# Local attention fused with a squared-ReLU layer: scores of four tiles joined in pairs, and a new order of work

## The chip, the core and the metric

The kernel runs on one core of a Trainium2 chip. A core has TensorE (PE; its weight loads have a row of their own, PEld), VectorE (DVE), ScalarE (ACT), GpSimd (POOL), SyncE (SP) and 16 DMA engines. Each engine takes its instructions in the order in which the program lists them, and waits on semaphores of the others. The metric is device time in microseconds, the median of several executions. Before the change it is 212.19 us (five runs, 211.66 to 212.37).

## The reference

For each of 4 batches and 8 heads (768 positions, head size 64), attention with a window, followed by a two-layer network over all 3072 rows:

```python
scores = scale * np.matmul(q, k.transpose(0, 1, 3, 2))
keep = is_global | is_local          # first 8 columns, or 0 <= row - column < 96
scores = np.where(keep, scores + bias[None], -1000000000.0)
a = np.exp(scores - max)             # then divided by its row sum
attn = np.matmul(a, v)               # -> x: 3072 rows of 512
r = np.maximum(x @ w_in, 0.0)        # w_in 512 x 2048
out = (r * r) @ w_out                # w_out 2048 x 512
```

## The kernel before, in words

**Tiling.** There are 24 tiles of 128 rows (six in each batch, numbered 0 to 23) and 12 blocks of two tiles each. A row sees its own tile, the tile to its left and the eight global columns, which a small DVE copy puts into the first columns of the left tile's keys (line 612, and line 683 for v). A batch's first tile (0, 6, 12, 18) has no left tile.

**Attention of a tile.** Queries and keys are loaded by POOL (line 211; q, k and v of a tile are three transfers that share POOL's queue), and transposed: on PE for tiles 0 to 5 (line 398, copied out of PSUM by lines 326 and 328), by a DMA transpose that SP issues from tile 6 on (line 422). Scores (line 485, `emit_sc`) are matmuls with a contraction of 64, one head each. Even and odd heads lie in the two halves of the array's rows, so the array is split, and an even and an odd head run side by side. A first tile has 8 of these matmuls and fills 2 PSUM banks; any other has 16 and fills 4. Then ACT takes the exponential (line 551, one instruction for each bank), DVE multiplies by mask and slope (line 576), PE multiplies by v (line 638, "pv", in two halves of four heads), DVE divides by the row sum (lines 665 and 666, "norm"), and x is transposed, by PE (line 701) for tiles below 8 and by a DMA transpose from SP (line 725) after that.

**The layer.** Block b and step s (eight of them) make one s1: 8 matmuls (line 753) into a PSUM bank hT. ACT applies the ReLU (line 774), DVE squares (line 786), and s2 adds it to the output tiles of the block (line 826, two matmuls for each step and tile). Finished tiles are copied out (lines 326 and 328) and stored by SP (line 865).

**PSUM.** Two of the eight banks hold s2's sums. The other six are one ring, taken in turn by scores, pv, transposes and s1. A PE operation that takes a bank waits until what was in it six banks ago has been read.

**What sets the order.** Each operation is entered in a `Plan` with a cost for its engine, its dependencies and a key. `Plan.run` places them one after the other, always the one that could start first, with 0.01 us for each unit of key (`URGE`), and the instructions are written to the engines in that order. The constants steer the keys: `SHIFT` by kind of operation, or by kind and tile, block or step; `LEADS` by how much a tile's attention runs ahead of the layer. `JOIN` holds pairs (tile, first group): such a tile's scores are no operation of their own, but are appended to the score operation before them (`joint`), so that they are issued in one stretch, which has the dependencies of both and takes the banks of both. `STEP` says after which s1 (counted through all blocks) a tile's scores may come; `HOLD` keeps the next s1 behind them.

Before the change, `JOIN` has tiles 15, 16, 18, 20, 21 and 23; their partners are the parts before them. Scores of tiles 6, 7, 11 and 12 are four stretches.

Of the kernel before, what the change touches and what calls it, by code (L numbers as in the profile page):

```python
# [21 lines left out]
class Plan:  # L22
# [8 lines left out]

    LAG = {"PE": 0.25, "ACT": 0.26, "DVE": 0.2, "SP": 0.6, "POOLQ": 0.8, "DMAQ": 1.2, "DMA": 0.0}
    URGE = 0.01
    SHIFT = {'T': -13, 'sc': -2.5, 'exp': -26, 'pv': -13, 'norm': -17, 'trx': -5, 'xT': 32, 'gk': -38, 'gv': -45, 'mul': -39, 'kl': 24, 's1': -3.5, 'relu': 8, 'sq': -13, 's2': -1.25, 'st': -30, ('mul', 4): 12, ('tr', 5): 18, ('T', 5): 8, ('norm', 5): -22, ('sc', 6): 16, ('pv', 6): 46, ('mul', 7): 29.5, ('gk', 7): -13, ('trx', 7): 12, ('sc', 8): -4, ('pv', 8): 9, ('norm', 9): -10, ('pv', 11): 14, ('pv', 12): 48, ('sc', 13): -14, ('pv', 14): 30, ('mul', 15): 17, ('norm', 17): 4, ('norm', 18): -36, ('exp', 19): -7, ('exp', 20): 14, ('pv', 20): 34, ('sc', 22): 10, ('s1', 2): -2.5, ('s1', 3): -32, ('sq', 3): 4, ('s1', 5): 9, ('s1', 6): 23.5, ('s1', 7): 34, ('s1', 8): -10, ('s2', 0): 7.5, ('s2', 2): -4, ('s2', 3): -27, ('s2', 4): 7.5, ('s2', 5): 22, ('s2', 6): 14, ('s2', 7): -4, ('s2', 8): -10, ('s2', 9): -8, ('s2', 10): -2}

    def shift(self, name):
        early = name[-1 if name[0] in ("T", "tr") else 1]
        return self.SHIFT.get(name[0], 0.0) + self.SHIFT.get((name[0], early), 0.0)

# [65 lines left out]
def kernel(  # L105
# [49 lines left out]
    def const(shape, dt, name):  # L155
        return consts.tile(shape, dt, name=name, tag=name)
# [18 lines left out]
    pbt = const([P, 2, P], FP32, "pbt")  # L175
    pbw = const([P, 2, P], FP32, "pbw")
    plan = Plan()
    LEADS = {5: 29.5, 6: 59, 7: 21, 8: 15, 9: 40, 10: 38, 11: 24, 12: 46, 13: 0, 14: 22, 15: 1, 16: -27, 17: 18, 18: -20, 19: 20, 20: 33, 22: 28, 23: 8}
    SAFE = {j: 1.6 for j in range(6, 12)} | {14: 4.2, 15: 3.2, 16: 3.5}
    SAFEX = {9: 1.5, 11: 1.5, 13: 2.5}  # L180


    SETS = {1: [(0,), (1,)], 2: [(0,), (1,)], 3: [(0,), (1,)], 15: [(0,), (1,)], 20: [(0,), (1,)], 23: [(0,), (1,)]}
    JOIN = {(21, 0), (16, 0), (23, 0), (18, 0), (20, 0), (15, 0)}
    COPY = [14, 15, 19, 20, 22]
    BEHIND = {}
    HOLD = ((6, 0), (19, 0))
    STEP = {(17, 0): 58, (19, 0): 68, (4, 0): -7, (6, 0): 16, (11, 0): 24, (12, 0): 37}
    JGATE = 11
    NHS = 14  # L190
    NWARM = 8
# [68 lines left out]
    def emit_ones(e, js):  # L260
        for j in js:
            nc.vector.memset(v_sb[j][:, :, D : D + 1], 1.0)
# [38 lines left out]
    for g in range(NFIRST + 2, NT, 6):  # L301
        js = range(g, min(g + 6, NT))
        o = plan.op(
            ("ones", g), {"DVE": 0.2}, lambda e, js=js: emit_ones(e, js),
            key=-1.0, ready=15.0,
        )
# [40 lines left out]
    kl = [const([P, NPAIR, P], BF16, f"kl_{i}") for i in range(2 if COPY else 0)]  # L347
# [8 lines left out]
    for j in range(NT):  # L356
        b, t = divmod(j, TPB)
        first = t == 0
        need = 8 * (j // 2)
        base = need - LEADS.get(j, LEAD) + 4 * (j % 2)  # L360
        if (j, 0) in JOIN:
            base -= 4
# [28 lines left out]
        for n in range(2) if j < JQK else ():  # L391
            users = []

            def emit_tr(e, j=j, n=n, fp=fp):
# [9 lines left out]
            tr = plan.op(  # L404
                ("tr", n, j), {"PE": 0.5 if fp else 0.24}, emit_tr,
                deps=[land["qk"[n], j]], key=base, takes=(*G, [users]),
            )
# [12 lines left out]
        if j >= JQK:  # L420
            def emit_dT(e, j=j, T_=T_):
# [5 lines left out]
            T = plan.op(  # L427
                ("T", j), {"SP": 1.3}, emit_dT,
                deps=[land["q", j], land["k", j], xT_op[j - 3]] + ku, key=base - 6,
            )  # L430
            T = plan.op(("moved", j), {"DMAQ": 1.2}, None, deps=[T])
            qk_users[slot(j)].append(T)
            if j in SAFE:

                T = plan.op(("seen", j), {"DMA": SAFE[j]}, None, deps=[T])
# [6 lines left out]
        mul, mul_users = {}, {}  # L442
# [55 lines left out]
        for gs in SETS.get(j, [tuple(range(groups))]):  # L498
            n = 8 * len(gs)
            sc_users = busers[2 * gs[0] : 2 * gs[-1] + 2]  # L500
            if (j, gs[0]) in JOIN:

                o, also, taken = joint
# [16 lines left out]
            if j < NBIAS:  # L520
# [6 lines left out]
            o = plan.op(  # L527
                ("sc", j, gs[0]), {"PE": 0.2 + 0.029 * n},
                lambda e, gs=also, f=emit_sc: f(e, gs), deps=[*deps, bias],
                key=base + 1 + 2 * gs[0], takes=takes,  # L530
            )
# [91 lines left out]
        norm = []  # L623
# [170 lines left out]
    for o in plan.ops:  # L794
        if o["name"][0] == "sc":
            j = o["name"][1]
            n = STEP.get(o["name"][1:], 4 * j - LEAD)
            if n >= 0 and j >= NFIRST:
                o["deps"].append(s1_ops[n // NSTEP, n % NSTEP])
                if o["name"][1:] in HOLD:  # L800
                    n += 1
                    s1_ops[n // NSTEP, n % NSTEP]["deps"].append(o)

    for blk in range(NBLK):
# [9 lines left out]
        for s, sub, half in order2:  # L814
# [5 lines left out]
            def emit_s2(e, blk=blk, s=s, sub=sub, half=half, w=w, cols=cols, own=own):  # L820
# [15 lines left out]
            o = plan.op(  # L836
                ("s2", blk, s, sub), {"PE": 0.43 * w / d_model}, emit_s2,
                deps=[d, land["wout", s]] + users[-1:],
                key=8 * blk + s + 2.0 + (0 if not last else 8 * sub + 8 * (half or 0)),
                takes=((*G, [users]) if own else ("acc", NACC, [users])) if s == 0 else None,  # L840
            )
# [6 lines left out]
            if s == NSTEP - 1:  # L848
# [14 lines left out]
                def emit_st(e, blk=blk, sub=sub, half=half, cols=cols):  # L863
# [7 lines left out]
                st = plan.op(  # L871
                    ("st", blk, sub), {"SP": 0.4}, emit_st,
                    deps=[ev, s1_ops[NLATE, 0] if blk < NLATE - 2 else None],
                    key=8 * blk + s + 9.0,
                )
                st = plan.op(("stored", blk, sub), {"DMAQ": 1.4}, None, deps=[st])
# [40 lines left out]
```

## Time and profile before

| | us |
|---|---|
| median of 5 runs | 212.19 |
| the profiled execution, its own time | 211.98 |
| its span, first to last instruction | 210.2 |
| PE busy | 203.2 |
| DVE busy | 143.2 |
| ACT busy | 119.4 |
| s1 matmuls (line 753), 768 | 94.2 |
| s2 matmuls (line 826), 376 in the records | 90.1 |
| exponentials (line 551), 78 with their mask on DVE | 40.4 |

The profile gives instructions with start and duration, the idle time of an engine ahead of an instruction with the engine that ended it ("waited for"), and a chain that is followed back from the last instruction. TensorE's granted clock was 1.00 in the whole span. PE's matmuls overlap, so that a row's duration is longer than what it adds: the step from the start of one matmul to that of the next is what counts. In the records, s1's matmuls follow each other at 109 ns, s2's at 216 ns, pv's at 29.5 ns. The program has 1984 matmuls and the profile 1960 records: where one of s2's is missing, a hole of 216 ns shows that is none.

### The profile page before, as it was taken

To read this page: it belongs to the slowest core of one execution; us is meant where nothing else is said; L and a number is where in the kernel's file an instruction comes from. 1 tells how busy PE (TensorE), PEld (TensorE's weight loads), DVE (VectorE), ACT (ScalarE), POOL (GpSimd) and SP (SyncE) were. 2 spreads that over 40 slices of the span, in tenths; PEclk is the share of its full clock that TensorE was granted. 3 is DMA by queue.
4 is the path that set the end of the run, shared out by engine and by line. 5 is a ranking of instruction groups with operands and counts; after the bars stand their busy time and mean duration, and the time that the engine had idled before them with its cause. 6 is when DMAs were issued, how large, how long until landed. Compare 5 with 4: busy or idle time off the path is not lost.

```text
span 210.2 us, 4998 instructions
## 1 busy us (share of the span) xinstructions
PE 203.2 (97%) x1960; PEld 142.0 (68%) x1984; DVE 143.2 (68%) x372; ACT 119.4 (57%) x222; POOL 73.8 (35%) x91
## 2 busy tenths in 40 slices
PE   7998999999999999999999999999999999999993
PEld 3686877666566856866856577587756766766862
DVE  7799688522887877884877684586786845944630
ACT  6886688134663754554754672755677436833531
POOL 8997765440637238213903150405500000000000
PEclk9999999999999999999999999999999999999999
DMA  8999999999799999999997979999973710410202
GB/s 127 149 177 187 184 191 200 176 179 223 76 172 135 201 120 162 190 145 138 159 155 76 218 72 97 143 133 113 136 133 75 176 27 3 125 27 3 100 0 100
DMA packets 112615, 27.32 MB, mean 130 GB/s; under 512 B 103248, under 2 KB 109648, under 8 KB 112592
## 3 DMA queue, kind: packets, MB, share of 16 engines
q0 software_dynamic: 79200, 13.37, 86.6%
q1 hardware_dynamic: 33392, 13.64, 33.6%
q8 instruction: 15, 0.25, 0.5%
q14 instruction: 8, 0.07, 0.1%
HBM read 27.26 MB, written 6.29 MB: 160 GB/s over the span
## 4 chain that ended last, share of the span: by engine, by line
PE 85%; POOL 5%; DMA 4%; DVE 2%; issue 1%; ACT 1%; POOLq 0%
PE acc L826 39%; PE hT L753 37%; PE sc L485 5%; PE po L638 4%; DMA win<-in_moe_w_in_dram 4%; POOL qk L211 3%; POOL v L211 2%; DVE x L666 1%; POOL win L211 1%; PE tr L398 0%; DVE hs L786 0%; DVE rs L665 0%; PE trx L701 0%; DVE at L576 0%; ACT hr L774 0%
## 5 line engine op out<-in xcount | busy, mean ns | idle before, releaser
L753 PE MATMUL hT<-xT,win 128*128 128x256 bf16 x768 | 94.2, 273 | 0.8 <-DMA win<-in_moe_w_in_dram 0.6
L826 PE MATMUL acc<-wout,hs 128*128 128x512 bf16 (+1 forms) x376 | 90.1, 370 | 1.3 <-DVE rs L665 0.2
L774 ACT ACTIVATE hr<-hT 128x512 f32<-128x512 f32 x96 | 57.3, 605 | 55.2 <-PE hT L753 46.8
L753 PEld LDWEIGHTS <-win 128*128 128x128 bf16 x768 | 73.5, 98 | 18.3 <-DMA win<-in_moe_w_in_dram 1.0
L786 DVE TENSOR_TENSOR hs<-hr 128x512 bf16<-128x512 f32 x96 | 65.1, 687 | 23.2 <-ACT hr L774 22.4
L826 PEld LDWEIGHTS <-hs 128*128 128x128 bf16 x400 | 36.8, 98 | 29.8
L551 ACT ACTIVATE esc<-sc 128x512 bf16<-128x512 f32 x78 | 40.4, 608 | 13.6 <-PE sc L485 13.0
L211 POOL DMA_DIRECT2D qk<-in_q_dram x23 | 20.7, 900 | 70.8 <-DMA qkT<-qk 53.4
L576 DVE TENSOR_TENSOR at<-esc,E 128x512 bf16<-128x512 bf16 x78 | 31.8, 422 | 8.6 <-ACT esc L551 6.3
L211 POOL DMA_DIRECT2D v<-in_v_dram x24 | 22.0, 915 | 1.4 <-DMA win<-in_moe_w_in_dram 1.0
L666 DVE TENSOR_TENSOR x<-po,rs 128x256 bf16<-128x256 f32 x48 | 20.4, 424 | 1.7
L211 POOL DMA_DIRECT2D qk<-in_k_dram x23 | 20.6, 899 | 0.5 <-DMA win<-in_moe_w_in_dram 0.5
L326 ACT COPY o<-acc 128x512 f32<-128x512 f32 (+1 forms) x20 | 11.2, 579 | 15.1 <-PE acc L826 15.0
L638 PEld LDWEIGHTS <-at 128*128 128x128 bf16 x352 | 15.6, 98 | 4.8 <-ACT at L551 0.2
L638 PE MATMUL po<-v,at 128*128 128x65 bf16 x352 | 17.3, 193 | 0.1
L665 DVE RECIPROCAL rs<-po 128x4 f32<-128x4 f32 x48 | 8.6, 178 | 10.4 <-PE po L638 9.8
L485 PEld LDWEIGHTS <-qkT 64*128 64x128 bf16 x312 | 9.5, 94 | 6.2 <-issue 5.5
L485 PE MATMUL sc<-qkT 64*128 64x128 bf16 x192 | 12.9, 219 | 0.1
L485 PE MATMUL sc<-qkT,qkT 64*128 64x128 bf16 x120 | 8.7, 216 | 0.0
L328 DVE COPY o<-acc 128x512 f32<-128x512 f32 x5 | 3.5, 692 | 6.9 <-PE acc L826 6.8
L612 DVE COPY qkT<-qkT 128x32 bf16<-128x32 bf16 x11 | 3.0, 271 | 5.8 <-PE sc L485 5.8
L211 POOL DMA_DIRECT2D win<-in_moe_w_in_dram x8 | 6.2, 806 | 1.4 <-issue 0.6
(45 smaller groups left out, 71.7 us busy)
## 6 DMA issues: line engine op xcount, KB each, us to landing
out_dram<-o SPq DMA_DIRECT2D x23, 256.0 KB, 3.7
v<-in_v_dram POOLq DMA_DIRECT2D x24, 128.0 KB, 6.4
qk<-in_q_dram POOLq DMA_DIRECT2D x23, 128.0 KB, 4.6
qk<-in_k_dram POOLq DMA_DIRECT2D x23, 128.0 KB, 5.8
win<-in_moe_w_in_dram POOLq DMA_DIRECT2D x8, 256.0 KB, 7.9
wout<-in_moe_w_out_dram POOLq DMA_DIRECT2D x8, 256.0 KB, 9.3
qkT<-qk SPq DMA_TRANSPOSE x18, 5.3
plain<-in_q_dram SPq DMA_DIRECT2D x1, 256.0 KB, 3.3
```

What stands on the lines that cost most here:

```text
L211: nc.gpsimd.dma_start(out=dst, in_=src)
L326: nc.scalar.copy(dst, src)
L485: nc.tensor.matmul(out=tiles["sc", j, odd, g][:, at, :], lhsT=left[j - 1][half, pair, :] if kt else qkT[j % NKT][half, 1, pair, :], rhs=qk ...
L551: nc.scalar.activation(out=esc, in_=tiles.pop(("sc", j, odd, g)).rearrange("p a c -> p (a c)"), func=Act.Exp, scale=scale,)
L576: nc.vector.tensor_mul(at, tiles.pop(("esc", j, odd, g)), bias)
L638: nc.tensor.matmul(out=po[:, hi, :], lhsT=tiles["at", j, odd, g][:, at * P : (at + 1) * P], rhs=v_sb[kj][:, h, :], start=(i == 0), stop=(i ...
L665: nc.vector.reciprocal(rs, po[:, :, D : D + 1])
L666: nc.vector.tensor_tensor(out=x[:, 4 * hf : 4 * hf + 4, :], in0=po[:, :, :D], in1=rs.to_broadcast([P, 4, D]), op=Alu.mult,)
L753: nc.tensor.matmul(out=hT[:, c, :], lhsT=w_in_sb[s][:, kt, c * P : (c + 1) * P], rhs=tiles["xT", blk][:, kt, :], start=(kt == 0), stop=(kt ...
L774: nc.scalar.activation(hr, tiles.pop(("hT", blk, s)), Act.Relu)
L786: nc.vector.tensor_mul(hs, hr, hr)
L826: nc.tensor.matmul(out=tiles["acc", blk, sub, half], lhsT=hs[:, c, sub * P : (sub + 1) * P], rhs=w_out_sb[s][:, c, cols], start=(s == 0 an ...
```

## The change

It touches constants alone. `JOIN` gains (7, 0) and (12, 0): scores of tile 7 follow those of tile 6, and those of tile 12 follow those of tile 11, in one stretch of 24 matmuls that takes all six banks of the ring. With it come other values in `SHIFT`, `LEADS`, `HOLD` and `STEP`, so that the whole order of work is another.

```diff
-    SHIFT = {'T': -13, 'sc': -2.5, 'exp': -26, 'pv': -13, 'norm': -17, 'trx': -5, 'xT': 32, 'gk': -38, 'gv': -45, 'mul': -39,
...
+    SHIFT = {'T': 47, 'sc': -5.25, 'pv': -2, 'norm': 26.5, 'trx': -2, 'xT': 51, 'gk': 42, 'gv': -127.5, 'mul': 24,
...
-    LEADS = {5: 29.5, 6: 59, 7: 21, 8: 15, 9: 40, 10: 38, 11: 24, 12: 46, 13: 0, 14: 22, 15: 1, 16: -27, 17: 18, 18: -20, 19: 20, 20: 33, 22: 28, 23: 8}
+    LEADS = {3: 51, 4: 17, 5: 16, 6: 27, 8: 2, 9: 20, 10: 42, 11: 47, 12: 0, 14: 0, 15: 7.5, 16: 34, 17: 46, 20: 28, 21: 15, 23: 56}
...
-    JOIN = {(21, 0), (16, 0), (23, 0), (18, 0), (20, 0), (15, 0)}
+    JOIN = {(7, 0), (12, 0), (21, 0), (16, 0), (23, 0), (18, 0), (20, 0), (15, 0)}
...
-    HOLD = ((6, 0), (19, 0))
-    STEP = {(17, 0): 58, (19, 0): 68, (4, 0): -7, (6, 0): 16, (11, 0): 24, (12, 0): 37}
+    HOLD = ((10, 0),)
+    STEP = {(4, 0): -7, (12, 0): 37, (5, 0): -2, (10, 0): 29, (13, 0): 30, (23, 1): 81}
```

Both programs have the same instructions on PE, SP and POOL, and POOL's stand in the same order. One copy of an output tile and one of an x tile go from DVE to ACT. In the new order PE has 21 stretches of scores in place of 24: the two that `JOIN` takes away, and one in the loading phase, where the two halves of tile 3's scores now stand side by side.

More of the change, by code (lines that the diff above doesn't have):

```diff
@@ L33 @@
     URGE = 0.01
-    SHIFT = {'T': -13, 'sc': -2.5, 'exp': -26, 'pv': -13, 'norm': -17, 'trx': -5, 'xT': 32, 'gk': -38, 'gv': -45, 'mul': -39, 'kl': 24, 's1': -3.5, 'relu': 8, 'sq': -13, 's2': -1.25, 'st': -30, ('mul', 4): 12, ('tr', 5): 18, ('T', 5): 8, ('norm', 5): -22, ('sc', 6): 16, ('pv', 6): 46, ('mul', 7): 29.5, ('gk', 7): -13, ('trx', 7): 12, ('sc', 8): -4, ('pv', 8): 9, ('norm', 9): -10, ('pv', 11): 14, ('pv', 12): 48, ('sc', 13): -14, ('pv', 14): 30, ('mul', 15): 17, ('norm', 17): 4, ('norm', 18): -36, ('exp', 19): -7, ('exp', 20): 14, ('pv', 20): 34, ('sc', 22): 10, ('s1', 2): -2.5, ('s1', 3): -32, ('sq', 3): 4, ('s1', 5): 9, ('s1', 6): 23.5, ('s1', 7): 34, ('s1', 8): -10, ('s2', 0): 7.5, ('s2', 2): -4, ('s2', 3): -27, ('s2', 4): 7.5, ('s2', 5): 22, ('s2', 6): 14, ('s2', 7): -4, ('s2', 8): -10, ('s2', 9): -8, ('s2', 10): -2}
+    SHIFT = {'T': 47, 'sc': -5.25, 'pv': -2, 'norm': 26.5, 'trx': -2, 'xT': 51, 'gk': 42, 'gv': -127.5, 'mul': 24, 'kl': 38.5, 'relu': 25.5, 'sq': 30, 's2': -5, 'o': 61, 'st': 78, ('mul', 3): 28, ('tr', 4): 10, ('xT', 5): -22, ('sc', 6): 14, ('pv', 7): -4, ('norm', 7): -17, ('trx', 7): -3, ('sc', 8): -12, ('pv', 8): -18, ('pv', 10): 45, ('sc', 11): 12, ('pv', 12): -50, ('sc', 13): 17, ('sc', 14): 6, ('pv', 14): 10, ('norm', 14): -28, ('sc', 15): -21, ('exp', 15): 20, ('exp', 16): 83, ('mul', 16): 92, ('norm', 16): -9, ('sc', 17): 32, ('pv', 17): 28, ('pv', 21): 9.5, ('pv', 22): -10, ('norm', 22): 8, ('s1', 2): -8.5, ('sq', 2): -10, ('relu', 3): 24, ('sq', 3): -82, ('s1', 5): 6, ('s1', 6): 30, ('sq', 6): 6, ('s1', 7): -6, ('sq', 7): -92, ('relu', 8): 40, ('s1', 9): -2, ('s1', 10): -10, ('s2', 0): 7.5, ('s2', 2): 1, ('s2', 4): -15, ('s2', 5): 37, ('s2', 6): -5, ('s2', 7): -3, ('s2', 9): 4.5, ('s2', 11): 30}
     def shift(self, name):
```

## The prediction

> **What bounds the kernel now.** I read the clock first (1.00 throughout), then PE's row in the slices, PE's waits, and PE's timeline around the score stretches.
>
> ```profile
> span 210.2 us, 4998 instructions
> ...
> PE   7998999999999999999999999999999999999993
> ```
>
> PE is full from the second slice to the last but one. The view of waits, cut to PE, lists everything that it waited for:
>
> ```profile
> PE warm L271 <- DVE zero L259: 1.2, 1, 1.2
> PE hT L753 <- DMA win<-in_moe_w_in_dram: 0.6, 1, 0.6
> PE tr L398 <- DMA qk<-in_k_dram: 0.2, 1, 0.2
> PE acc L826 <- DVE rs L665: 0.2, 1, 0.2
> PE acc L826 <- DVE qkT L612: 0.2, 1, 0.2
> ```
>
> The first three lie before 20 us. The last two are holes of one s2 matmul (216 ns) where the profile lacks a record, so they are no waits. The last true wait ends here, in PE's timeline; its columns are start, length, instructions:
>
> ```profile
> 18.64 1.05 PE L753 MATMUL hT<-xT,win 128*128 128x256 bf16 x8 [0.62 <-DMA win<-in_moe_w_in_dram]
> 19.52 0.39 PE L701 MATMUL trx<-ident,x 128*128 128x128 bf16 x4
> 19.98 1.05 PE L753 MATMUL hT<-xT,win 128*128 128x256 bf16 x8
> ```
>
> These are s1 of block 0, steps 2 and 3, each held by its piece of w_in. By the records step 3's piece lands at 19.93; PE is done with the transposes at 19.74, so it stands 0.24 us. From 19.98 to the last s2 (207.0) I checked each start against the one before it at the rates of 109, 216, 56 and 29.5 ns: beyond holes of missing records nothing is left, except one cost that comes with each stretch of scores. So the end is set by 19.98 plus PE's work, plus the last copy and store (207.03 to 210.2).
>
> **The price of a stretch.** A stretch of 16 (tile 7) and one of 8 (tile 6), with the rows around them:
>
> ```profile
> 56.02 0.59 PE L826 MATMUL acc<-wout,hs 128*128 128x512 bf16 x2
> 56.54 0.23 PE L485 MATMUL sc<-qkT 64*128 64x128 bf16 x2
> ...
> 56.94 0.22 PE L485 MATMUL sc<-qkT,qkT 64*128 64x128 bf16 x2
> 57.10 0.40 PE L701 MATMUL trx<-ident,x 128*128 128x128 bf16 x4
> ```
>
> ```profile
> 49.70 1.04 PE L753 MATMUL hT<-xT,win 128*128 128x256 bf16 x8
> 50.67 0.40 PE L485 MATMUL sc<-qkT 64*128 64x128 bf16 x8
> 51.00 1.47 PE L826 MATMUL acc<-wout,hs 128*128 128x512 bf16 x6
> ```
>
> The two s2 matmuls from 56.02 are done at 56.02 + 2 x 0.216 = 56.45, the next full-array work starts at 57.10: 0.65 us for 16. For 8: 49.70 + 8 x 0.109 = 50.57, to 51.00: 0.43. The records, to the ns, give 0.648, 0.425, and 0.872 for the six stretches of 24. So eight more cost 0.224, and a stretch costs 0.425 - 0.224 = 0.20 for going in and out; 0.011 comes on top, because the first matmul after a stretch is that much slow. **One stretch less is worth 0.21 us**, if it was on PE's full part.
>
> **The change part by part.**
>
> 1. *Two stretches less after 19.98.* The built orders, laid side by side, have 17 stretches there before and 15 after: 6 with 7, and 11 with 12, are one each. 2 x 0.21 = 0.42 us saved. Counts on PE are the same and the rates too.
>
> 2. *One stretch less before 19.98* (tile 3's halves). Its 0.21 us ends in the wait for w_in: POOL's list is the same, so step 3's piece lands at 19.93 again. Gain 0. If that cover were gone, by an earlier landing, up to 0.2 more; if the new order there made PE late, a loss. That order puts all 18 small memsets ahead of the second half of tile 2's norm (in the profile six take 0.27 us, so 0.81). By the rows (mask 0.34 apart, reciprocal 0.2, norm 0.34), tile 3's x is ready near 19.2, and PE wants it at 19.51: 0.3 spare. Taken: 0.
>
> 3. *The added wait: a joined stretch needs both tiles' keys and all six banks, and everything on PE queues behind it.* Keys: counting the new order's work from 19.98, the stretch 6+7 stands at 52.2; the DMA transpose of tile 7 lands at 50.2 in the records, 2 us earlier. 11+12 stands at 85.9; tile 12's transpose landed at 82.3. Banks: the last s1 ahead of 6+7 ends 3.1 us before it, ahead of 11+12 1.3 us; a ReLU takes 0.61. Taken: 0.
>
> 4. *After the joined stretch* six exponentials stand on ACT. The six stretches of 24 of the old order show the case: at 119.47 PE goes on with three s2 steps (1.3 us, no ring bank) and starts s1 at 120.77 without a gap, while ACT works through the exponentials:
>
> ```profile
> 119.12 2.56 ACT L551 ACTIVATE esc<-sc 128x512 bf16<-128x512 f32 x5 [1.02 <-PE sc L485]
> ```
>
> That is 0.51 us for each bank. The new order has the same three s2 steps behind both joined stretches. Without that cover PE would wait for the first bank until 119.12 + 0.60, some 0.3 us in each stretch, 0.6 in all. Here a rule speaks against the change: the Trainium skill, TensorEngine Tiling (Array Packing), section PSUM Bottleneck, says that tiling speeds up TensorE but not the evacuation of PSUM, and that the PSUM copy may become the bottleneck. Were PE to wait for all six banks, this would make 6 x 0.51 - 1.3 = 1.8 us a stretch, 3.5 in all; the rows show one bank is enough at a time. Taken: 0.
>
> 5. *The rest of the order.* Shortest way from s1 over ReLU and square to its s2: 1.84 us of PE work lie between (block 7, step 7), 1.94 before (block 11, step 7). It needs 0.60 + 0.69 and hand-offs, 1.35 to 1.5 us. With the queues of ACT and DVE laid out by the same rows (exponential 0.53, mask 0.34, norm 0.54, square 0.61, start to start), pv of tiles 12, 19, 20 and 22 and an s2 of block 8 are spared by 0.03 to 0.2 us. Bounds: nothing, or 0.1 to 0.2 us at up to four places, 0.8 at most. I take 0, as the old order's shortest one shows no wait.
>
> 6. *SP and the DMA queues.* SP has the same 61 issues; from block 6 on, stores stand singly between transposes instead of in pairs. A store waits for its copy out of PSUM and holds what is queued behind it: key transposes of tiles 19 and 21 among it, which then still have 17 and 12 us until their scores. What PE waits for here is x: from the last pv of a block's second tile to the block's first s1 over norm, SP and the DMA. PE work between these (start to start) in blocks 4 to 11: before 7.6, 9.6, 11.1, 7.7, 5.7, 6.8, 13.2, 6.3; after 7.4, 7.2, 10.2, 7.7, 6.5, 6.5, 6.3, 9.8. The smallest grows from 5.7 to 6.3. In the records SP issues 1.15 us after that pv starts (86.70 to 87.85, block 5). The landing takes what this row says (us min/median/max, x transposes):
>
> ```profile
> DMA to landing us min/median/max: 2.4/3.7/7.5
> ```
>
> Where the loads are over, it takes 2.4 to 3.6 by the records (blocks 9 to 11). Blocks 4 and 5 lie where the DMA engines are full; they have 6.2 and 6.0 us. The same two transposes took 3.5 and 5.7 there. I take no wait: in the new order tile 9's loads and transposes run some 3 us earlier, so the jam that held them is over sooner.
>
> **Sum.** The profiled execution: 211.98 - 0.42 = 211.56 (span 209.8). It lies 0.21 under the median of the runs, so for the median 212.19 - 0.42 = 211.77, say **211.8**, 0.20% less. PE was without a gap, so there is nothing else to win.
>
> **Rivals.**
>
> A (the forecast): no new wait, 211.8.
>
> B: small waits in item 5 and the loading phase eat the gain. For it: spare times of 0.1 to 0.3 in several places. Against it: equal spare times waited for nothing in the old order. 0.2 to 0.8 of waits: 212.0 to 212.6.
>
> C (slower): x of block 5 or 4 lands late. Both fall in the full stretch of the DMA row, and block 5's room shrinks from 9.6 to 7.2. From a landing of 6.0 us on it costs one for one, and all PE work stands behind. At the 7.5 of the row: 1.5 us for block 5, 1.3 for block 4; net +1.1 for one, +2.4 for both: 213.3 to 214.6. Against it: 5.7 in the old order, behind a key transpose that landed just before it (93.1 and 93.5).
>
> D: the change gains more, because the loading phase ends earlier too (w_in's pieces land 0.1 to 0.3 us sooner): 211.5.
>
> E: `JOIN` does nothing, as an operation comes in between: the built order excludes it.
>
> **How the numbers follow.** A 0.62, B 0.16, C 0.15, D 0.07. The measurement of this kernel can tell about 0.2% (0.42 us) from no change, and A lies on that edge: I split it 0.32 faster, 0.30 within. B: 0.11 within, 0.05 slower. C slower. D faster. So faster 0.39, within 0.41, slower 0.20. The median of five runs lies some 0.2 us around its place (the runs spread over 0.7), so A alone is 211.5 to 212.1. The range reaches to 211.4 for D, and above through B to the lower part of C, 212.8; what is left out is most of C and some of A's and D's tails.
>
> **What would show it.** Right: step 3 of block 0 at 19.98 again; 15 stretches after it, those of 6+7 and 11+12 with 0.87 us each; no wait of PE after 20 us; the last s2 ended by 206.6. Wrong: PE waiting in s1 (line 753) for a DMA transpose or for x at block 4 or 5 (C); PE waits for squares, masks or norms (B); step 3 at another time than 19.98 (D, or item 2's loss).

## The result, and the profile after

The changed kernel takes **211.89 us** (median of 53 runs, 211.04 to 214.55), the kernel before 212.33 (95 runs beside them). The ratio is 0.9980, 95% interval 0.9971 to 0.9989: 0.42 us less (0.23 to 0.62). The forecast was 211.8 and 0.42 less. Only the runs of the result are as many as this; the experiments have 4 to 12 each, so their ratios are good to some 0.2%, and what separates them is read from PE's records, which are good to a few ns.

The first lines of the page after, and PE's row in the slices, are as full as before:

```profile
span 210.1 us, 4976 instructions
...
PE   7898999999999999999999999999999999999993
```

The view of waits, cut to PE (in all, times, longest; us):

```profile
PE warm L271 <- DVE zero L259: 1.2, 1, 1.2
PE tr L398 <- DMA plain<-in_k_dram: 0.8, 1, 0.8
PE hT L753 <- DMA win<-in_moe_w_in_dram: 0.7, 2, 0.4
PE acc L826 <- issue: 0.3, 2, 0.2
PE acc L826 <- DVE hs L786: 0.2, 1, 0.2
PE acc L826 <- DVE qkT L612: 0.2, 1, 0.2
```

As before, the first three lie ahead of 20 us and the last three are holes of a missing s2 record. In PE's timeline, w_in's pieces hold s1 of block 0 as they did, but both steps come earlier (step 3 at 19.80; in the kernel before it was at 19.98):

```profile
18.44 1.05 PE L753 MATMUL hT<-xT,win 128*128 128x256 bf16 x8 [0.43 <-DMA win<-in_moe_w_in_dram]
...
19.80 1.70 PE L753 MATMUL hT<-xT,win 128*128 128x256 bf16 x14
```

The joined stretch of tiles 11 and 12, in the same view, and ACT's timeline beside it:

```profile
86.14 0.23 PE L485 MATMUL sc<-qkT 64*128 64x128 bf16 x2
...
86.60 0.39 PE L485 MATMUL sc<-qkT 64*128 64x128 bf16 x8
86.92 1.47 PE L826 MATMUL acc<-wout,hs 128*128 128x512 bf16 x5
88.22 1.04 PE L753 MATMUL hT<-xT,win 128*128 128x256 bf16 x8
```

```profile
86.57 3.05 ACT L551 ACTIVATE esc<-sc 128x512 bf16<-128x512 f32 x6 [1.02 <-PE sc L485]
```

From the end of the s2 before it (86.05) to the s2 after it (86.92) the stretch takes 0.87 us, as foretold, and the three steps of s2 (five of six records are there) lead without a gap to the s1 at 88.22, while ACT is still busy with the exponentials until 89.6.

**The ledger that the rest goes by.** "PE's part" is the time from s1 of block 0, step 3, to the start of the last s2 matmul. Steps from start to start that are longer than the rate of their kind are waits; a stretch of scores costs 0.21.

| kernel | step 3 at | PE's part | stretches | waits in it |
|---|---|---|---|---|
| before | 19.98 | 186.74 | 17 | 0 |
| after | 19.80 | 186.78 | 15 | 0.49 |
| after, profiled again (below) | 19.77 | 186.30 | 15 | 0 |

So the first profile of after holds both: two stretches less, worth 0.45 (186.74 less 186.29, which is 186.78 without its waits), and three waits that the view of waits doesn't list, as they are short or lie beside a missing record: 0.11 and 0.12 at 37.3 and 38.3 (a piece of w_out landed at 37.60, then v of tile 5), and 0.25 at 145.27, where s1 of block 8 starts after its x landed at 145.42, 5.57 us after SP issued it.

### The profile page after: what moved, and what is told of

It reads as the page before. It is cut to its first block, busy times and chain, and to the rows that moved or that the text cites. A ratio compares the mean times of both kernels' runs of the same rounds, so it can differ in the third digit from the quotient of the medians.

```text
span 210.1 us, 4976 instructions
## 1 busy us (share of the span) xinstructions
PE 202.0 (96%) x1957; PEld 141.6 (67%) x1984; DVE 140.5 (67%) x370; ACT 120.2 (57%) x224; POOL 73.8 (35%) x91
## 4 chain that ended last, share of the span: by engine, by line
PE 85%; POOL 5%; DMA 4%; DVE 2%; ACT 2%; issue 1%; POOLq 0%
PE acc L826 38%; PE hT L753 37%; PE sc L485 5%; PE po L638 4%; DMA win<-in_moe_w_in_dram 4%; POOL qk L211 3%; POOL v L211 2%; ACT esc L551 1%; POOL win L211 1%; DVE x L666 1%; DVE hs L786 1%; PE trx L701 1%; PE tr L398 1%; DVE rs L665 0%; DVE v L683 0%
## 5 line engine op out<-in xcount | busy, mean ns | idle before, releaser
L826 PE MATMUL acc<-wout,hs 128*128 128x512 bf16 (+1 forms) x373 | 87.2, 370 | 1.7 <-issue 0.3
L826 PEld LDWEIGHTS <-hs 128*128 128x128 bf16 x400 | 37.4, 98 | 33.2 <-issue 0.2
L551 ACT ACTIVATE esc<-sc 128x512 bf16<-128x512 f32 x78 | 39.9, 611 | 12.6 <-PE sc L485 12.6
L576 DVE TENSOR_TENSOR at<-esc,E 128x512 bf16<-128x512 bf16 x78 | 32.4, 424 | 10.6 <-ACT esc L551 7.8
L328 DVE COPY o<-acc 128x512 f32<-128x512 f32 x4 | 2.8, 691 | 6.2 <-PE acc L826 6.2
L211 POOL DMA_DIRECT2D wout<-in_moe_w_out_dram x8 | 5.8, 719 | 1.9 <-DMA win<-in_moe_w_in_dram 1.1
```

Of the source, the lines that this page charges most:

```text
L211: nc.gpsimd.dma_start(out=dst, in_=src)
L551: nc.scalar.activation(out=esc, in_=tiles.pop(("sc", j, odd, g)).rearrange("p a c -> p (a c)"), func=Act.Exp, scale=scale,)
L576: nc.vector.tensor_mul(at, tiles.pop(("esc", j, odd, g)), bias)
L826: nc.tensor.matmul(out=tiles["acc", blk, sub, half], lhsT=hs[:, c, sub * P : (sub + 1) * P], rhs=w_out_sb[s][:, c, cols], start=(s == 0 an ...
```

## The experiments

My theory was the forecast's: the gain is two entries into and exits from the split array, 0.21 us each, and the rest of the order is worth nothing. Rivals: the gain comes from the new order or from the loading phase; the two stretches saved more, and the waits of the profile ate a part of it in every run.

**1. The changed kernel again**, unaltered.

> The changed kernel, unaltered, as the yardstick for the runs beside it and for a second profile. Price theory (two stretches less on PE's full part are worth 0.42 us): 0.42 us under the kernel before, ratio 0.998. If the two waits of the first profile (0.23 us at s2 steps 5 and the pv of tile 5 for w_out's pieces and v, 0.25 us at the first s1 of block 8 for x) belong to the order, both stand in this profile too, within 0.1 us; if they are chance of the DMA queues, at least one is gone or moved by more than 0.2 us.

Measured: 211.81, ratio 0.9983 (0.9960 to 1.0005). PE's part is 186.30 us with no wait: 0.44 less than before's 186.74. The three waits of the first profile are gone, so they come and go from one execution of the same program to the next; in the first profile each ended with the landing of a DMA.

**2. The two new stretches opened again.** The order of after, but one step of s2 (two matmuls) is put between tiles 6 and 7, and between 11 and 12. The rest of the stretch (`rest`) is issued behind the next PE operation, which is that step:

```diff
+    OPEN = {(6, 0), (11, 0)}
...
+        if o["name"][0] == "sc" and o["name"][1:] in OPEN:
+            f, gs = o["parts"][0]
+            f("PE", gs)
+            rest = o["parts"][1:]
...
+        if rest and o["engine"] == "PE":
```

> The changed kernel with the two new stretches opened again and nothing else moved: the second tile's part (tile 7's, tile 12's) is issued behind one s2 step of two matmuls. Price theory: 2 x 0.21 = 0.42 us slower than the changed kernel, so about as long as the kernel before (ratio 1.000, 0.998 to 1.002), and 17 stretches after the first 20 us in the profile. Rival (the gain came from the new order and not from the joints): no slower than the changed kernel, ratio 0.998.

Measured: 212.12, ratio 0.9991 (0.9974 to 1.0008). PE's part 186.72, no wait, 17 stretches: 0.42 above the run before, and 0.02 from the kernel before. PE's timeline shows two stretches in place of one (the edit adds a line above, so line 827 is line 826 of the other kernels):

```profile
53.29 0.40 PE L485 MATMUL sc<-qkT 64*128 64x128 bf16 x8
53.62 0.60 PE L827 MATMUL acc<-wout,hs 128*128 128x512 bf16 x2
54.16 0.23 PE L485 MATMUL sc<-qkT 64*128 64x128 bf16 x2
```

The whole new order, without the two seams, is thus worth nothing (186.72 against 186.74). By the times alone this kernel and the changed one can't be told apart (0.9991 and 0.9983, each good to 0.2%).

**3. The same edit on the kernel before, at six places**, to have the price larger than the noise:

```diff
+    OPEN = {(14, 0), (15, 1), (17, 0), (19, 0), (20, 1), (22, 0)}
```

> The kernel before with its six stretches of 24 opened in the same way, each by one s2 step: three times the dose. Price theory: 6 x 0.21 = 1.27 us slower than the kernel before, ratio 1.006 (1.004 to 1.008). Rival (the cost of going in and out lies beside other work or waits anyway): under 0.4 us, ratio below 1.002.

Measured: 213.48, ratio 1.0052 (1.0034 to 1.0069), 23 stretches. PE's part is 188.52, of which 0.52 are waits for w_out and v (0.07 at 35.6 and 0.45 at 38.6 us), so that waits of this kind are nothing peculiar to the new order:

```profile
PE po L639 <- DMA v<-in_v_dram: 0.3, 1, 0.3
```

Without them 188.00, or 1.26 above before: 0.21 for each of six. The times (0.52% of 212.4, or 1.1 us) bear out that separate stretches cost, and PE's records give the size.

**4. The cover taken away.** In after, s1 is put straight behind the joined stretches of 11+12, 14+15 and 19+20, and the steps of s2 that stood between come behind it:

```diff
+    HEAD = {(12, 0): ("sc", 11, 0), (15, 0): ("sc", 14, 0), (20, 0): ("sc", 19, 0)}
...
+        while done[spot]["name"][0] != "s1":
+            if done[spot]["engine"] == "PE":
...
+                later.append(done.pop(spot))
+            else:
+                spot += 1
...
+        done[spot + 1 : spot + 1] = later
```

> The changed kernel, but behind the three joined stretches of tiles 11+12, 14+15 and 19+20 the next s1 comes at once, and the s2 steps that stood between (three to five of them) follow it. Theory: s1 needs the bank of the first exponential alone, so PE waits 0.25 to 0.35 us each time, 0.75 to 1.05 us in all, ratio to the kernel before 1.002 to 1.003. Rival 1 (PE needs all six banks read): 6 x 0.51 - 0 = 3 us each, 9 us in all, ratio 1.04. Rival 2 (the bank is free in time, the cover is not needed): as the changed kernel, 0.998.

Measured: 213.02, ratio 1.0022 (0.9995 to 1.0049); PE's part 188.39, of it 2.14 of waits. The view of waits has the three new ones in one row, and PE's timeline shows the first:

```profile
PE hT L753 <- ACT esc L551: 1.1, 3, 0.7
```

```profile
87.19 0.39 PE L485 MATMUL sc<-qkT 64*128 64x128 bf16 x8
87.81 1.03 PE L753 MATMUL hT<-xT,win 128*128 128x256 bf16 x8 [0.23 <-ACT esc L551]
```

By the starts the three are 0.302, 0.302 and 0.749 us. PE waits for the first of the six banks alone: its s1 starts at 87.81, 0.05 us after the first exponential (87.16 to 87.76) is over, while the next ones are still to come (2.06 us for four of the six). So rival 1, 3 us for each stretch, is out, and so is rival 2, no wait at all. The third wait is more than was expected, because the first exponential of the stretch 19+20 starts late. These are PE's last pair and s1, and ACT's row; behind them ACT's row of the same stretch in the kernel before:

```profile
152.45 0.22 PE L485 MATMUL sc<-qkT,kl 64*128 64x128 bf16 x2
153.35 0.82 PE L753 MATMUL hT<-xT,win 128*128 128x256 bf16 x6 [0.68 <-ACT esc L551]
```

```profile
152.70 1.57 ACT L551 ACTIVATE esc<-sc 128x512 bf16<-128x512 f32 x3 [1.47 <-PE sc L485]
```

```profile
152.06 3.05 ACT L551 ACTIVATE esc<-sc 128x512 bf16<-128x512 f32 x6
```

ACT had nothing to do for 1.47 us and began 0.03 us after the end of the last of the 24 matmuls (152.67), where in 11+12 it began as the first eight were over (87.13). The order of work is the reason: in the new order `Plan.run` lists the exponentials of tile 20 ahead of those of tile 19 on ACT, and tile 20's scores are the last eight of the stretch. In the kernel before, tile 19's came first, and ACT began at 152.06, 0.25 us before the last matmul ended (152.31). The changed kernel has the late start as well (151.32, the last matmul's end at 151.28), but under its cover of s2 steps. The other 0.79 of waits are DMAs: 0.32 for w_out and v, 0.47 for x of block 8, which landed 5.79 us after its issue.

**5 and 6. Each half of the change alone.** Before with the two new pairs in `JOIN` and nothing else; after without them:

```diff
-    JOIN = {(21, 0), (16, 0), (23, 0), (18, 0), (20, 0), (15, 0)}
+    JOIN = {(7, 0), (12, 0), (21, 0), (16, 0), (23, 0), (18, 0), (20, 0), (15, 0)}
```

> The kernel before with the two new pairs in JOIN and every other constant as it was, so that the plan finds its order with the old steering values. Theory (the joints pay 0.42 us and a new order has to be found that makes room for them): slower. Its order, laid out by the rows, has the x of block 5 some 4 us late and those of blocks 7 and 8 some 1.5 us each, and squares, copies and masks 0.5 to 1.6 us late in four places: 4 to 9 us slower than the kernel before, ratio 1.02 to 1.04, and waits of PE on x and DVE in the profile. Rival (the joints alone bring the gain): ratio 0.998.

> The changed kernel without the two new pairs in JOIN, all other new constants kept. Theory (the values were found for the joined stretches and steer another order without them): slower than before by 5 to 10 us, ratio 1.025 to 1.05, most of it at block 5, whose x the laid-out order has 4 to 6 us late. Rival (the new values are the better ones by themselves, and the joints add to them): ratio 0.998 to 1.000.

Measured: the pairs alone took 218.54 us in the one run at a granted clock of 0.999, 6.4 us more than the kernel before, and 223.83 to 226.13 in three runs at 0.984 or 0.985; one run is too few for a ratio. Their profile is one of the three: in it the granted clock was 0.50 in two stretches of 3.41 us, from 102.22 and from 153.42 us on, beside PE's two long waits for x (until 102.66 and 152.63). The order alone took 219.72, ratio 1.0353 (1.0335 to 1.0371), 7.5 us slower. The views of waits show where it goes; first the pairs alone, then the order alone:

```profile
PE hT L753 <- DMA xT<-x: 5.6, 2, 3.2
...
```

```profile
PE acc L826 <- DVE hs L786: 2.5, 3, 1.3
PE hT L753 <- DMA xT<-x: 2.0, 2, 1.3
...
PE po L638 <- DVE v L683: 0.9, 1, 0.9
PE po L638 <- DVE at L576: 0.8, 1, 0.8
```

PE waits for x (in the first near 99 and 150 us), for squares, masks and v. The sizes are about as expected, the places only in part: with the pairs alone the x of blocks 5 and 8 was late and that of block 7 was not, and with the order alone the x of block 5, which was to be most of it, cost 0.80 of 7.9 us. `JOIN` and the constants are one setting: changing one set reshuffles the list that `Plan.run` writes, and then s1, s2 and pv stand too close behind what they need. In the order of after the same two joins bring no wait (run 1).

**7. The loading phase.** In after, pv of tile 2's second half goes between tile 3's halves again, as before:

```diff
+    pv = done.pop(at("pv", 2, 1))
+    done.insert(at("sc", 3, 1), pv)
```

> The changed kernel with the third of its saved stretches opened: the second half of tile 2's pv stands between the halves of tile 3's scores again, as before the change. Theory of the prediction (this one lies behind the wait for w_in and is worth nothing): as the changed kernel, ratio 0.998, within 0.1 us of it, and the s1 of block 0, step 3 starts when its piece of w_in lands. Rival: 0.21 us slower than the changed kernel.

Measured: 211.61 (6 runs), ratio 0.9972 (0.9953 to 0.9991); step 3 at 19.58, PE's part 186.29, no wait. The third stretch that the change saves is worth nothing. Step 3 did not start with the landing of its piece, as expected: the piece had landed at 19.42, and PE came from step 2, which its own piece held until 18.47, and the transposes behind it. The opened stretch lies ahead of that wait.

**8 to 10. The waits of the first profile.** Two edits on after: the loads of tile 22 on POOL come behind the first s1 of block 8, so that they do not stand in the queues with block 8's x; and s1 of block 1, step 7, comes ahead of the s2 that had waited for w_out. A small write on DVE (`gate22`) holds the loads back. First both, then each alone:

```diff
+    load22 = done.pop(at("load", 22))
...
+    spot22 = at("s1", 8, 0)
+    done[spot22 + 1 : spot22 + 1] = [dict(name=("gate", 22), engine="DVE", emit=gate22), load22]
...
+    s1_17 = done.pop(at("s1", 1, 7))
+    done.insert(at("s2", 0, 5, 0), s1_17)
```

> The changed kernel with two moves against the waits that its first profile showed: the loads of tile 22 are held by a small memset on DVE until the first s1 of block 8 has been issued, so that the x of tile 17 does not share the queues with them, and the s1 of block 1, step 7 goes ahead of the s2 of step 5, which gives w_out's last pieces and tile 5's v 0.87 us more. If the two waits are frequent (as in two profiles of three: 0.5 and 0.8 us, none in the other), 0.1 to 0.5 us faster than the changed kernel, ratio 0.996 to 0.9975, and neither wait in the profile. Rival (they are rare, or what is moved makes a wait elsewhere): as the changed kernel or slower, 0.998 or more.

> One half of the run before: the loads of tile 22 alone are put behind the first s1 of block 8, the rest is the changed kernel. Theory 1 (the wait of 0.25 to 0.47 us for x of block 8 comes, in those profiles that show it, from the loads of tile 22 that stand in the DMA queues ahead of its transpose): the transposes of x of block 8 land 2.4 us after their issue and PE doesn't wait for them; PE's part from step 3 of block 0 to the last s2 is 186.3, 15 stretches; time that of the changed kernel or up to 0.3 us less, 211.5 to 211.9 beside 212.2 to 212.4 before, ratio 0.996 to 0.998. Theory 2 (the 0.8 us which the run before lost came with these late loads): PE waits at tile 22 or in the stretch of its scores, ratio 1.000 to 1.002.

> The other half: step 7 of block 1's s1 alone goes ahead of s2's step 5 of block 0. Theory 1 (this edit cost the run before its 0.65 us of waits, since the second half of tile 5 then starts its way over norm later and the transposes on PE that read it come as early as before): waits of 0.4 to 0.7 us in the transposes near 40 us, PE's part 186.7 to 187.0, time 212.2 to 212.6, ratio 1.000 to 1.002. Theory 2 (it was the late loads, or chance of that run): no waits near 40 us, PE's part 186.3, ratio 0.996 to 0.998.

Measured:

| kernel | median | ratio (95%) | PE's part | waits in it | landing of block 8's x |
|---|---|---|---|---|---|
| both | 212.63 | 1.0022 (1.0003 to 1.0040) | 186.97 | 0.65 | 2.41 |
| late loads alone | 211.62 | 0.9958 (0.9934 to 0.9981) | 186.30 | 0 | 2.41 |
| early s1 alone | 212.46 | 0.9999 (0.9975 to 1.0023) | 186.97 | 0.65 | 3.67 |

The loss comes from the early s1. PE's timeline, in after and with the early s1 alone:

```profile
38.81 0.47 PE L638 MATMUL po<-v,at 128*128 128x65 bf16 x10
39.12 1.03 PE L753 MATMUL hT<-xT,win 128*128 128x256 bf16 x8
39.99 0.38 PE L826 MATMUL acc<-wout,hs 128*128 128x512 bf16 x1
40.42 0.39 PE L701 MATMUL trx<-ident,x 128*128 128x128 bf16 x4
```

```profile
39.67 0.65 PE L638 MATMUL po<-v,at 128*128 128x65 bf16 x16
40.16 0.38 PE L826 MATMUL acc<-wout,hs 128*128 128x512 bf16 x1
40.81 0.28 PE L701 MATMUL trx<-ident,x 128*128 128x128 bf16 x2 [0.28 <-DVE x L666]
41.36 0.29 PE L701 MATMUL trx<-ident,x 128*128 128x128 bf16 x2 [0.26 <-DVE x L666]
```

In after that s1 stands between pv of tile 5 and the transposes of its x, and covers the norm on DVE. Moved ahead, it leaves two matmuls of s2 there (one is missing in the records), and PE waits twice. The late loads do what they were to do. Before the first s1 of block 8 there are 5.3 us from issue to need; x landed in 5.57, 4.07, 5.27, 5.79, 3.71 and 3.67 us in the six profiles with the loads of tile 22 where after has them (kernels after, 1, 2, 4, 7, 10), so it was late in two; it landed in 2.41 in both with late loads. Which of the six it is goes with the moment of tile 22's first load: POOL issued it 0.64 to 0.69 us ahead of x's transpose in the two late ones (5.79 and 5.57), at the same time in the one of 5.27, and 0.15 to 0.20 ahead in the three of 3.67 to 4.07. The median of the late loads alone, 211.62, is the lowest but for one, and its interval overlaps that of after: whether it is faster is not settled.

## Why the prediction was right

1. **Two stretches less, 0.42 us: right.** 0.44 by PE's part in the profile without waits (186.30), 0.42 when the seams were opened, 0.21 apiece at six others.
2. **The loading phase, 0: right, but for the reason's fixed point.** The forecast had step 3 at 19.98 again. It came at 19.80, and in the other profiles at 19.50 to 20.88. That w_in's piece sets it is right: in all profiles but that of run 7, step 3 starts 0.04 to 0.05 us after its piece has landed. But the landing moves by up to 1.2 us between executions with the same order up to there, and where PE waits for nothing else the end moves with it. The forecast holds nonetheless, since it compares medians; whether the new order shifts the landing by less than this spread, the profiles can't tell.
3. **The added wait, 0: right.** Keys of tile 7 landed at 50.77, the stretch began at 52.44; tile 12's landed at 81.74, its stretch began at 86.14. The rooms are 1.7 and 4.4 us, foretold as 2.0 and 3.6.
4. **Exponentials behind the stretch, 0 under the cover and 0.3 without: right.** No gap in after, 0.302 twice without the cover. The other end of this step was the Trainium skill's page TensorEngine Tiling (Array Packing), section PSUM Bottleneck: copying out of PSUM, which tiling does not make faster, may become the bottleneck (the page says so of TensorE made four times faster; here the array is split in two). Evacuation does hold PE once the cover is gone, but by 0.30 in these two, not by the 3 us that all six banks would have cost without cover (1.8 us with it, by the forecast): PE waited for one bank. Start to start the exponentials are 0.48 to 0.49 us apart, not 0.51, which changes nothing here. What was not seen is the 0.75 behind 19+20, where the new order puts tile 20's exponentials first.
5. **The rest of the order, 0: right in the typical run.** PE's part is the same with the seams opened (186.72 and 186.74). None of the places of 0.03 to 0.2 us spare waited in either profile of after. What waited at 37.3 and 38.3 in the first was a piece of w_out and v, which the item did not name.
6. **The DMA queues, 0: right in sum, with the wrong block watched.** Blocks 4 and 5, where rival C had its place, landed in 3.79 and 2.41 us: no wait. Block 8's room, 6.5 us less 1.15 to the issue, was in the list, and it is there that x was late, by 0.25, in the first profile, and by 0.47 in one more. I had looked at where the DMA engines are full on average, not at which loads are queued at that moment.

**The rivals.** B's size (0.2 to 0.8 of small waits) appeared in the first profile, 0.49, though from DMAs and not from norms or squares, and not in the second; the median over 53 runs, 0.42 less, leaves little room for it in the typical run. C did not occur. D did in the profile (0.18 earlier), which the spread of step 3 makes chance. Settled, by PE's records: the gain is the two seams, the ways into and out of a stretch, since it goes when they are opened and nothing else is moved. Left open: how often the waits of 0.25 to 0.5 us come.

## What to carry to other kernels

Where an engine is full, count what each change of its mode costs from the records (here 0.21 us for going into and out of a stretch on the split array), and multiply; then look for what covers the added wait, and move that cover away in an experiment to see its price. A short gap in one profile is to be seen again in a second before it is explained or repaired: one repair here cost more than the wait, because the instruction that was moved had been the cover of another. In a list scheduler with tuned constants, half of a setting is no smaller step: it was 7.5 us slower here, for a change worth 0.4.

## What the runs showed of the hardware

- Step 3 of block 0 starts at 19.64 to 20.88 us in the eight profiles whose order up to there is that of after (after, 1, 2, 4, 6, 8, 9, 10), a spread of 1.2 us; PE's part behind it repeats to 0.01 us where nothing waits (186.30, 186.29 and 186.30 in the kernels of 1, 7 and 9).
- The same DMA transpose (x of block 8) landed in 2.41 us with no load queued beside it, and in 3.67 to 5.79 with the loads of tile 22 under way.
- Going into and out of a stretch on the split array costs 0.20 us: 8, 16 and 24 matmuls take 0.425, 0.648 and 0.872 us, so that eight more cost 0.224. The first matmul after it takes 0.011 more. Beyond waits and missing records, this held in all stretches of the ledger.
- The weight loads (PEld) show where these 0.20 us lie. In the kernel before, ahead of the stretch of tile 6, s1's weights are loaded 0.108 us before their matmul starts (50.361 and 50.469), but the first scores' weights 0.005 us before theirs (50.669 and 50.674), and those of the s2 behind the stretch 0.004 (50.999 and 51.003). So each of the two seams adds some 0.1 us:

```profile
50.67 0.23 PEld L485 LDWEIGHTS <-qkT 64*128 64x128 bf16 x8 [0.21 <-issue]
51.00 0.55 PEld L826 LDWEIGHTS <-hs 128*128 128x128 bf16 x4
```

From s1 to s2, and between these and pv or transposes, PE's records show no such step. No run tells whether the split is the reason or something else about the scores.
